# Layer one's first product by seven half-width products in blocks 2 to 5, with the weights for it fetched piece by piece into two buffers

## The chip, the cores and the metric

One core of a Trainium2 chip runs the kernel. The metric is the device time of one execution in microseconds; less is better. The core's engines work at the same time, each through its own instructions in a fixed order: PE (TensorE, matrix products), DVE (VectorE), ACT (ScalarE), POOL (GpSimd) and SP, which here only issues transfers; ACT issues some as well. An engine that meets an instruction whose inputs or buffer are not ready waits, and so does all that stands behind it.

## The reference

Attention with a decay per head, in a running state, and then two feed-forward layers over all 3072 tokens (4 sequences of 768):

```python
for t in range(S):
    state = gamma[None, :, None, None] * state + np.einsum('bhd,bhe->bhde', k[:, :, t], v[:, :, t])
    y[:, :, t] = scale * np.einsum('bhd,bhde->bhe', q[:, :, t], state)
x = y.transpose(0, 2, 1, 3).reshape(B * S, H * D)
h = x @ moe_w_in;  x = np.maximum(0.01 * h, h) @ moe_w_out
h = x @ moe2_w_in; out = (h * np.cos(h)) @ moe2_w_out
```

The model width is 512 (8 heads of 64), the inner width of both layers 2048. All is float32.

## The kernel before

**Numbers in two parts.** Every operand of a large product is split into a high part that TensorE takes exactly and a low part. A product is then three matmuls (`mm3`, L360): high by high, low by high, high by low. A high part is a copy on ACT (`high_g`, L510), a low part a subtraction on DVE or POOL (`low_g`, L515). Layer weights come as 64-bit words, from which ACT, DVE and POOL make the two parts in four steps (`exponent`, `fraction`, `top_bits`, `round_up`, L123 to L139).

**Tiling.** The tokens form six blocks of 512 (`NB`, `BLK`), the inner width 16 tiles of 128 (`NF`), the model width 4 (`KD`). Attention goes by 24 units of 128 tokens (`C`), four to a block. A unit's matmuls (`excursion`, L406) use the PSUM banks p1 and p2 for the next unit's scores and state, and p3 for this unit's output.

**Layer one** is the loop over `SEGMENTS` (L765): blocks 0 and 1 in two parts each, while the weights are being made, then blocks 2 to 5 whole. For each tile f, `gemm1` (L487) multiplies the block by 128 columns of the first weights, 4 x 3 matmuls of 512 columns into one bank; ACT applies the slope (`Leaky.begin`, L502); `high_g` and `low_g` give the pair g; and some tiles later `gemm2_a` (L715) adds g times the second weights to four accumulators, 12 matmuls of 512 columns. The attention units of block n + 1 lie in block n (`block_steps`), two steps to a tile.

**Layer two** is the loop over 24 quads (L952). It multiplies pairs of token blocks and pairs of tiles by Strassen's seven products, `P1` to `P7`: seven products of sums of parts take the place of eight, and DVE adds the results together. The seven sums of weights for pair p are made ahead (`pair_at`, L603, `pair_sums`, L287), kept in DRAM (`w2i`) and fetched into the two large buffers b0 and b1 (`load_wi`, L351).

**What sets the order.** The order on each engine is that of the program. The preparation of layer two's weights and inputs is spread over blocks 2 to 5 by `Agenda` (L215): a step stands at a moment, and `tick` runs the moments, two to a tile. Transfers are nearly all issued by SP, in that order.

Of the kernel before, what the change touches and what calls it, by code (L numbers as in the profile page):

```python
# [60 lines left out]
XMADE = ("P1", "P2", "P3", "P5", "P7", "P6", "P4")  # L61

# [17 lines left out]
def body(ctx: ExitStack, tc: tile.TileContext, att, first, w1, w2, out):  # L80
# [128 lines left out]
    xq = [[dpool.tile([P, 1024], F32, name=f"xq{s}_{i}") for i in range(14)] for s in range(1, NB // 2)]  # L209
# [87 lines left out]
    def xprep(agenda, m, s, xlow=None, step=13):  # L297
# [9 lines left out]
        for k in range(2):  # L307
            way = {}
            for i, name, keep in ((0, "P1", True), (1, "P2", True), (3, "P3", True), (0, "P5", False), (2, "P7", False), (3, "P6", False), (1, "P4", False)):
                j = 7 * k + XMADE.index(name)  # L310
                if s == 0:
                    way[name] = parts(place(i), partial(own_x, j), 0, xlow or nc.vector, keep, None)
                else:
                    way[name] = parts(place(i), xq[s - 1][j], 0, nc.vector, keep, ostage, False)
# [17 lines left out]
    def load_xq(s, j):  # L332
        assert ("x", s) in made
        xt[j] = w_tile(j, 0, F32R, 1024)
        nc.sync.dma_start(out=xt[j].bitcast(F32), in_=xq[s - 1][j])

    def own_x(j):
        if j not in xt:
            xt[j] = w_tile(j, 0, F32R, 1024)
# [9 lines left out]
    wi = {}  # L349

    def load_wi(p, place):  # L351
        assert ("p", p) in made
# [127 lines left out]

    def new_x(n):
# [37 lines left out]
    with tc.manual_schedule():  # L519

        with ExitStack() as pctx, ExitStack() as actx:
# [4 lines left out]
            xs = {}  # L526
# [11 lines left out]
            def evacuate(u):  # L538
                n = u // CPB
                if n not in xs:  # L540
# [8 lines left out]
            def unit_steps(u):  # L549
                def both():  # L550
# [3 lines left out]
                    heads.lower[u](nc.gpsimd)  # L554
# [12 lines left out]
                return [both, int, state, int, values, int, int, int]  # L567

            def block_steps(n):
                return [step for u in range(n * CPB, n * CPB + CPB) for step in unit_steps(u)]  # L570

            agenda = Agenda()
            START, LAST = 4, 2 * (NF * (NB - 3) - 4)
            m, turn = 0, 0
# [4 lines left out]
            def raw2():  # L582
                return cbuf[:, 0:2, :].rearrange("p a n -> p (a n)")

            def begin(f, part):
                return lambda: fetch2(raw2(), f, part)

            def half(f):
# [453 lines left out]
```

## Time and profile before

| what | us |
|---|---|
| median of 3 runs | 1099.12 (1098.64 to 1100.45) |
| the profiled execution | 1098.76 |
| its span, first to last instruction | 1096.9 |
| PE busy | 1080.1 (98%) |
| DVE busy | 658.9 (60%) |
| ACT busy | 484.3 (44%) |
| POOL busy | 179.7 (16%) |

The stages of the profiled execution: the start up to 35 us, blocks 0 and 1 to 219.5, blocks 2 to 5 to 595, layer two to the end. Busy shares are means over these stages. Matmuls overlap in the records, so the distance from one start to the next tells more of them than how long each lasts. The chain of work is followed backwards from the last instruction, at each step to what released it; an engine with a large share of it sets the time. Transfers move 189 MB in all.

### The profile page before, as it was taken

How to read it: one execution, taken by the hardware profiler on the slowest of the kernel's cores; microseconds unless marked ns; L12 is line 12 of the kernel's file. 1: busy time of each engine (PE TensorE's matmuls, PEld its weight loads, DVE VectorE, ACT ScalarE, POOL GpSimd, SP SyncE). 2: the span in 40 equal slices, each digit the busy share in tenths (PEclk: the TensorE clock that was granted, in tenths of full speed). 3: DMA queues.
4: the chain of work that ended last, by engine and by line, in shares of the span. 5: the costliest groups of instructions: out<-in, count | busy, mean ns of one | idle time of the engine just before them, and what ended most of it. 6: DMA issues, size and time to landing. Idle time of an engine off the chain costs nothing.

```text
span 1096.9 us, 18667 instructions
## 1 busy us (share of the span) xinstructions
PE 1080.1 (98%) x7484; PEld 897.4 (82%) x7484; DVE 658.9 (60%) x1003; ACT 484.3 (44%) x826; POOL 179.7 (16%) x146
## 2 busy tenths in 40 slices
PE   6899999999999999999999999999999999999998
PEld 6788888888888888888888888888888888888887
DVE  4788843123544535343786777877667877656665
ACT  3468732223434434343553555544445544444432
POOL 3210011112534333341464000000000000000000
PEclk9999999999999999999999999999999999999999
DMA  8646433133646445433795446585446495413412
GB/s 314 237 147 229 163 92 101 41 116 118 195 134 219 145 154 183 154 106 115 249 332 187 156 162 239 172 308 211 161 168 240 159 329 199 163 68 146 167 43 77
DMA packets 71082, 189.22 MB, mean 173 GB/s; under 512 B 7891, under 2 KB 10195, under 8 KB 70995
## 3 DMA queue, kind: packets, MB, share of 16 engines
q1 hardware_dynamic: 67536, 175.44, 46.1%
q10 hardware_dynamic: 3456, 12.58, 3.4%
q8 instruction: 59, 0.97, 0.4%
q14 instruction: 31, 0.23, 0.1%
HBM read 135.57 MB, written 52.43 MB: 171 GB/s over the span
## 4 chain that ended last, share of the span: by engine, by line
PE 96%; DMA 3%; issue 0%; ACT 0%; POOL 0%; SPq 0%; ACTq 0%; DVE 0%; POOLq 0%
PE p L361 19%; PE p L363 19%; PE p L362 19%; PE acc L361 12%; PE acc L362 12%; PE acc L363 12%; PE p L412 3%; DMA w<-att 2%; PE p L415 1%; DMA vs<-att 0%; PE acc L412 0%; ACT vp L400 0%; POOL vp L402 0%; PE p L492 0%; PE p L493 0%
## 5 line engine op out<-in xcount | busy, mean ns | idle before, releaser
L361 PE MATMUL acc<-g,w 128*128 128x512 f32 x384 | 151.3, 394 | 0.0
L363 PE MATMUL acc<-g,w 128*128 128x512 f32 x384 | 149.6, 390 | 0.0
L362 PE MATMUL acc<-g,w 128*128 128x512 f32 x384 | 149.6, 389 | 0.0
L361 PE MATMUL p<-b,w 128*128 128x512 f32 x380 | 148.1, 390 | 0.0
L363 PE MATMUL p<-b,w 128*128 128x512 f32 x380 | 147.8, 389 | 0.0
L362 PE MATMUL p<-b,w 128*128 128x512 f32 x380 | 147.8, 389 | 0.0
L361 PE MATMUL p<-w,b 128*128 128x512 f32 x336 | 130.7, 389 | 0.0
L362 PE MATMUL p<-w,b 128*128 128x512 f32 x336 | 130.7, 389 | 0.0
L363 PE MATMUL p<-w,b 128*128 128x512 f32 x336 | 130.7, 389 | 0.0
L516 DVE TENSOR_TENSOR g<-t,g 128x512 fp32r<-128x512 f32 x96 | 84.7, 885 | 53.4 <-ACT g L512 53.4
L504 ACT ACTIVATE t<-p 128x512 f32<-128x512 f32 x96 | 57.3, 597 | 121.8 <-PE p L363 114.4
L361 PEld LDWEIGHTS acc<-g,w 128*128 128x128 f32 x384 | 72.1, 188 | 15.6
L363 PEld LDWEIGHTS acc<-g,w 128*128 128x128 f32 x384 | 72.1, 188 | 15.2
L362 PEld LDWEIGHTS acc<-g,w 128*128 128x128 f32 x384 | 72.1, 188 | 14.6
L363 PEld LDWEIGHTS p<-b,w 128*128 128x128 f32 x380 | 71.3, 188 | 14.9
L362 PEld LDWEIGHTS p<-b,w 128*128 128x128 f32 x380 | 71.3, 188 | 14.8
L361 PEld LDWEIGHTS p<-b,w 128*128 128x128 f32 x380 | 71.3, 188 | 14.8
L512 ACT CAST g<-t 128x512 fp32r<-128x512 f32 x96 | 59.4, 619 | 53.5 <-PE acc L363 53.2
L860 ACT ACTIVATE k<-d,bias 128x512 int32<-128x512 f32 x24 | 17.4, 726 | 141.9 <-DVE d L847 141.9
L865 ACT ACTIVATE r<-r,bias 128x512 f32<-128x512 f32 x96 | 69.6, 725 | 18.4 <-DVE r L862 18.4
L362 PE MATMUL p<-w,w 128*128 128x512 f32 (+1 forms) x196 | 75.4, 385 | 0.0
L363 PE MATMUL p<-w,w 128*128 128x512 f32 (+1 forms) x196 | 75.4, 385 | 0.0
(133 smaller groups left out, 2043.3 us busy)
## 6 DMA issues: line engine op xcount, KB each, us to landing
b<-w2i SPq DMA_DIRECT2D x60, 512.0 KB, 5.7
w<-w2d SPq DMA_DIRECT2D x32, 512.0 KB, 8.1
w<-xq SPq DMA_DIRECT2D x28, 512.0 KB, 5.5
cbuf<-w SPq DMA_DIRECT2D x24, 512.0 KB, 4.0
xq<-o SPq DMA_DIRECT2D x40, 256.0 KB, 2.3
vs<-att SPq DMA_DIRECT2D x17, 512.0 KB, 3.8
w<-w SPq DMA_DIRECT2D x16, 512.0 KB, 10.1
w<-w ACTq DMA_DIRECT2D x16, 512.0 KB, 4.6
```

The source lines that it names most:

```text
L361: nc.tensor.matmul(o, sh, mh, start=start, stop=False)
L362: nc.tensor.matmul(o, sl, mh, start=False, stop=False)
L363: nc.tensor.matmul(o, sh, ml, start=False, stop=stop)
L412: return lambda: nc.tensor.matmul(out, stationary, moving, start=True, stop=True)
L415: return lambda start, stop: nc.tensor.matmul(out, stationary, moving, start=start, stop=stop)
L504: nc.scalar.activation(out=t, in_=hp, func=AF.Prelu, alpha=0.01)
L512: nc.scalar.copy(out=pair[:, 0], in_=g)
L516: eng.tensor_tensor(out=pair[:, 1], in0=g, in1=pair[:, 0].bitcast(F32), op=ALU.subtract)
L860: nc.scalar.activation(out=k, in_=h, func=AF.Identity, bias=bias[:, 0:1], scale=1.0)
L865: nc.scalar.activation(out=r, in_=r, func=AF.Sin, bias=bias[:, 1:2], scale=TURN)
```

## The change

In blocks 2 to 5 the tiles are taken in pairs, and layer one's first product is computed as layer two's is: by seven products, here of 256 columns (half a block of tokens), each 2 x 3 matmuls. `first_layer(i)` does pair i of 32; DVE adds the results in two tiles of the tag `t`, ACT applies the slope there, and POOL makes the low part for one of the two tiles of a pair. The bank pairs in `WHERE` put two products into each bank, and odd pairs use the banks in another order than even ones.

What this needs is made elsewhere. `first_pair` makes the sums of layer one's weights for a pair of tiles, from the parts already in SBUF, in blocks 0 and 1, and keeps them in DRAM (`w1i`). `x_steps` makes the seven sums of a block's inputs; for it the attention units of blocks 2 to 5 leave their tokens unsplit (`plain_tokens`). `follow` and `load_wi` fetch the weights of pair i + 2 in four pieces on ACT's queue, after pair i, into eight tiles of the first weights that are no longer needed; layer two's weights go the same way. Pairs run forwards in one block and backwards in the next, so that two pairs at each turn stay.

The agenda has four moments to a pair; the units and the steps of `x_steps` stand at moments of their own (`plan`). Six pairs of layer two's weights instead of four are made up to block 4, from two buffers by turns, with the low parts on DVE. The inputs of layer two's first two blocks go in part through DRAM and are fetched at the end of block 5, and layer two's input and weight tiles change places. The core of the diff:

```diff
+HALF = BLK // 2
+WHERE = ({"P1": (0, 0), "P6": (0, 1), "P7": (1, 0), "P5": (1, 1), "P2": (3, 0), "P4": (3, 1), "P3": (2, 0)},
+         {"P1": (1, 0), "P6": (1, 1), "P7": (3, 0), "P5": (3, 1), "P2": (0, 0), "P4": (0, 1), "P3": (2, 0)})
+WSLOTS = ((2, 3, 4, 5), (9, 10, 11, 12))
+RAW = (0, 1)
+XSLOTS = ((6, 7, 8), (13, 14, 15))
+XSHARED = {0: (("P1", 0), ("P1", 1), ("P6", 0), ("P6", 1)), 1: (("P4", 0), ("P4", 1), ("P3", 0), ("P3", 1))}
+XLATE = (*XSHARED[1], ("P2", 1))
+XALONE = {("P7", 0): 0, ("P7", 1): 1, ("P5", 0): 6, ("P5", 1): 7, ("P2", 0): 8, ("P2", 1): 13}
...
+    turns = [("a", pair_of(q)) for q in range(NQ * (NB - 2))] + [("p", pair_of(q)) for q in range(NQ * NB // 2)]
+
+    def follow(i, eng=nc.sync):
+        if i + 2 < len(turns) and turns[i + 2] not in wi:
+            return load_wi(turns[i + 2], wi[turns[i]][1], eng)
+        return []
+
+    def load_wi(key, place, eng=nc.sync):
+        assert key in made
         for old in [o for o in wi if wi[o][1] == place]:
             del wi[old]
-        t = xpool.tile([P, 4096], F32R, tag=f"b{place}", name=f"b{place}")
-        wi[p] = t, place
-        for lo, hi in ((0, 1024), (1024, 2048), (2048, 3072), (3072, WIN)):
-            nc.sync.dma_start(out=t[:, lo:hi].bitcast(F32), in_=w2i[p][:, lo:hi])
+        src = (w1i if key[0] == "a" else w2i)[key[1]]
+        tiles = []
+        wi[key] = tiles, place
+
+        def piece(i):
+            n = min(1024, WIN - 1024 * i)
+            t = w_tile(WSLOTS[place][i], 0, F32R, 1024)
+            eng.dma_start(out=t[:, :n].bitcast(F32), in_=src[:, 1024 * i : 1024 * i + n])
+            tiles.append(t)
+
+        return [partial(piece, i) for i in range(4)]
...
+        def plain_tokens(self, u, raw, tok0):
+            for j in range(2):
+                nc.vector.tensor_tensor(
+                    out=raw[j].rearrange("p (k n) -> p k n", k=2)[:, :, tok0 : tok0 + C],
+                    in0=self.po[u][:, j * 256 : j * 256 + 256].rearrange("p (k n) -> p k n", k=2),
+                    in1=self.tb[:, O_Q + j * 256 : O_Q + j * 256 + 256].rearrange("p (k n) -> p k n", k=2),
+                    op=ALU.mult,
+                )
...
+            when = {8: -37, 9: -28, 10: -21, 11: -15}
+            plan = {}
+            for u in range(2 * CPB, NU):
+                t = when.setdefault(u, 8 * (u - 3 * CPB) - 2)
+                both, state, values = unit_steps(u)
+                plan.setdefault(t, []).append(both)
+                plan.setdefault(t + 1, []).append(state)
+                plan.setdefault(t + 2, []).append(values)
+            for n in range(2, NB):
+                t = when[n * CPB + 3]
+                for at, fn in zip((-7, -4, 2, 3, 4, 4, 6) if n > 2 else (3, 4, 6, 10, 10, 10, 11), x_steps(n)):
+                    plan.setdefault(t + at, []).append(fn)
...
-                first, mid, last = rounding(raw2, t)
-                high, low = parts(t, w2d[f], 0, nc.gpsimd, False, ostage)
-                for i, step in zip((0, 2, 3, 3, 4, 5), (begin(f, 1), first, mid, last, high, low)):
+                first, mid, last = rounding(partial(raw2, turn), t)
+                high, low = parts(t, w2d[f], 0, nc.vector, False, ostage)
+                for i, step in zip((1, 3, 4, 5, 5, 6), (begin(f, 1, turn), first, mid, last, high, low)):
...
+                def plain():
+                    send(w1i[p][:, 0:1024], w()[0].bitcast(F32), False)
+                    for i in range(2):
+                        send(w1i[p][:, 3072 + 256 * i : 3328 + 256 * i], w()[1][:, 256 + 512 * i : 512 + 512 * i].bitcast(F32), False)
+
+                def whole():
+                    for i in range(2):
+                        sub2(held(i), w()[i][:, :512], w()[i][:, 512:], ALU.add)
+
+                highs = late_fn(lambda: w_tile(2 * p, 0, F32, 1024) if way == "own" else heads.first)
+
+                def room(i):
+                    return lambda n: highs()[:, 512 * i : 512 * i + 512]
+
+                g2 = parts(partial(held, 0), w1i[p], 1024, nc.gpsimd, False, room(0), False)
+                g3 = parts(partial(held, 1), w1i[p], 2048, nc.vector, False, room(1), False)
+                agenda.put(b, plain, whole)
+                agenda.put(b + 1, lambda: pair_sums(held(0), held(1)))
+                agenda.put(b + 2, g2[0], g3[0])
+                agenda.put(b + 3, g2[1], g3[1], lambda: made.add(("a", p)))
...
+            for p, (b, way) in enumerate(zip((-42, -26, -20, -23, -18, -16, -14, -7), ("own", "own", 3, 0, 1, 2, 4, 5))):
+                first_pair(p, b - 2 * START, way)
+            agenda.put(-6 - 2 * START, lambda: at_once(load_wi(("a", 0), 0)))
+            agenda.put(-7 - 2 * START, lambda: at_once(load_wi(("a", 1), 1)))
...
+            def first_layer(i):
+                n, q = 2 + i // NQ, i % NQ
+                key = turns[i]
+                p = key[1]
+                first, second = (stage("t") for _ in range(2))
+                a, b, c, d = first[:, :HALF], first[:, HALF:], second[:, :HALF], second[:, HALF:]
+                banks = {}
+
+                def product(name):
+                    at, half = WHERE[q % 2][name]
+                    if half == 0:
+                        banks[at] = bank(at)
+                    o = banks[at][:, half * HALF : half * HALF + HALF]
+                    x = xin[n, name]
+                    for k in range(2):
+                        h, l = w_part(key, name, k)
+                        mm3(o, h, l, x[:, k * HALF : k * HALF + HALF], x[:, 512 + k * HALF : 512 + k * HALF + HALF], k == 0, k == 1)
+                    if (n, q) == (NB - 1, NQ - 1) and name == "P5":
+                        load_xq(0, "P3", 1)
+                    if (n, q) == (NB - 1, NQ - 1) and name == "P2":
+                        load_xq(0, "P2", 1)
+                    return o
+
+                def moment(j):
+                    at = 4 * i + j
+                    for step in plan.pop(at, ()):
+                        step()
+                    flush()
+                    agenda.run(at - 2 * START)
+                    at_once(arriving[j : j + 1])
+
+                def add(out, o, s):
+                    nc.vector.tensor_tensor(out=out, in0=o, in1=s, op=ALU.add)
+
+                def slope(t):
+                    nc.scalar.activation(out=t, in_=t, func=AF.Prelu, alpha=0.01)
+
+                def ready(t, g, f, k):
+                    pending.append((gemm2_q, n, f, low_g(t, g, nc.gpsimd if k else nc.vector), (q, k) == (0, 0), (q, k) == (NQ - 1, 1)))
+
+                p1, p6 = product("P1"), product("P6")
+                nc.vector.tensor_copy(out=a, in_=p1)
+                add(b, p6, a)
+                p7, p5 = product("P7"), product("P5")
+                add(c, p7, b)
+                add(d, p5, c)
+                add(b, p5, b)
+                p2, p4 = product("P2"), product("P4")
+                add(a, p2, a)
+                add(c, p4, c)
+                slope(second)
+                add(b, product("P3"), b)
+                arriving = follow(i, nc.scalar)
+                g = high_g(second)
+                slope(first)
+                moment(0)
+                fn, *args = pending.pop(0)
+                fn(*args)
+                ready(second, g, 2 * p + 1, 0)
+                moment(1)
+                moment(2)
+                while len(pending) > 1:
+                    fn, *args = pending.pop(0)
+                    fn(*args)
+                ready(first, high_g(first), 2 * p, 1)
+                moment(3)
```

How this changes the order at three places. PE in block 2 ahead of the change, where one tile's first product ends and a second product of block 1, two tiles late, begins:

```order
1051 L361 MATMUL p_2644<-b_1880,w_0_684 128x512
1052 L362 MATMUL p_2644<-b_1880,w_0_684 128x512
1053 L363 MATMUL p_2644<-b_1880,w_0_684 128x512
1054 L361 MATMUL acc_2077<-g,w_1_1776 128x512
1055 L362 MATMUL acc_2077<-g,w_1_1776 128x512
1056 L363 MATMUL acc_2077<-g,w_1_1776 128x512
```

PE in the first pair of block 2 now, from P4 to P3 (`p_2808` is the bank of P2 and P4, `p_2824` that of P3):

```order
1027 L413 MATMUL p_2808<-w_0_2626,w_0_2603 128x256
1028 L414 MATMUL p_2808<-w_0_2626,w_0_2603 128x256
1029 L415 MATMUL p_2808<-w_0_2626,w_0_2603 128x256
1030 L413 MATMUL p_2824<-w_0_2529,w_0_2599 128x256
1031 L414 MATMUL p_2824<-w_0_2529,w_0_2599 128x256
1032 L415 MATMUL p_2824<-w_0_2529,w_0_2599 128x256
```

Where 12 matmuls of 512 columns stood for each tile, 42 of 256 columns stand for two tiles, and a second product follows only behind all seven. DVE in block 3 ahead of the change, from one low part of g (L516) to the next unit's mask (L448); L129 and L134 work on layer two's weights:

```order
281 L516 TENSOR_TENSOR g<-t,g 128x512
282 L129 TENSOR_SCALAR cbuf<-cbuf 128x512
283 L134 SCALAR_TENSOR_TENSOR cbuf<-cbuf 128x512
284 L461 TENSOR_TENSOR state<-p_3676,state 128x256
285 L516 TENSOR_TENSOR g<-t,g 128x512
286 L129 TENSOR_SCALAR cbuf<-cbuf 128x512
287 L134 SCALAR_TENSOR_TENSOR cbuf<-cbuf 128x512
288 L516 TENSOR_TENSOR g<-t,g 128x512 x2
289 L129 TENSOR_SCALAR cbuf<-cbuf 128x512
290 L134 SCALAR_TENSOR_TENSOR cbuf<-cbuf 128x512
291 L448 TENSOR_TENSOR sf<-p_3909,first 128x512
```

DVE in an early pair of block 2 now: the eight operations of the seven products (L1047, L1038), then the low part (L577), an attention unit and layer two's weights:

```order
306 L1047 COPY t<-p_3216 128x256
307 L1038 TENSOR_TENSOR t<-p_3216,t 128x256
308 L1038 TENSOR_TENSOR t<-p_3231,t 128x256 x3
309 L1038 TENSOR_TENSOR t<-p_3247,t 128x256 x2
310 L1038 TENSOR_TENSOR t<-p_3263,t 128x256
311 L138 TENSOR_SCALAR cbuf<-cbuf 128x512
312 L143 SCALAR_TENSOR_TENSOR cbuf<-first,cbuf 128x512
313 L577 TENSOR_TENSOR g<-t,g 128x512
314 L500 TENSOR_TENSOR sf<-p_3298,first 128x512
315 L513 TENSOR_TENSOR state<-p_3299,state 128x256
316 L535 TENSOR_TENSOR w_0_2748<-p_3300,first 128x2x128
317 L535 TENSOR_TENSOR w_0_2749<-p_3300,first 128x2x128
```

Eight short operations on PSUM have come in for each pair, with one low part of g between them instead of two. ACT around one fetch of layer two's weights (L124 and L126 are its first steps) ahead of the change:

```order
264 L512 CAST g<-t 128x512
265 L504 ACTIVATE t<-p_3528 128x512
266 L124 ACTIVATE cbuf<-cbuf 128x512
267 L126 ACTIVATE cbuf<-cbuf 128x512
268 L512 CAST g<-t 128x512
269 L504 ACTIVATE t<-p_3567 128x512
270 L268 CAST o<-cbuf 128x512
271 L706 ACTIVATE o<-acc_2701 128x512
```

ACT in the first pair of block 2 now (L1041 is the slope, L573 a high part, L398 a piece of weights from `w1i`):

```order
214 L1041 ACTIVATE t<-t 128x512
215 L573 CAST g<-t 128x512
216 L1041 ACTIVATE t<-t 128x512
217 L398 DMA w_0_2838<-w1i_118 128x1024
218 L398 DMA w_0_2861<-w1i_118 128x1024
219 L133 ACTIVATE cbuf<-cbuf 128x512
220 L135 ACTIVATE cbuf<-cbuf 128x512
221 L398 DMA w_0_2865<-w1i_118 128x1024
222 L573 CAST g<-t 128x512
223 L398 DMA w_0_2905<-w1i_118 128x512
```

The pieces of layer one's weights stand between the steps of layer two's weights, and some of them behind L133, which waits for a fetch.

## Rows read from the trace of the kernel before

**Rows 1.** Busy time on the page: busy us (share of the span) x instructions.
```profile
PE 1080.1 (98%) x7484; PEld 897.4 (82%) x7484; DVE 658.9 (60%) x1003; ACT 484.3 (44%) x826; POOL 179.7 (16%) x146
```

**Rows 2.** Shares of the chain that ended last, on the page, by engine.
```profile
PE 96%; DMA 3%; issue 0%; ACT 0%; POOL 0%; SPq 0%; ACTq 0%; DVE 0%; POOLq 0%
```

**Rows 3.** PE's waits from 60 us on: total us, times, longest.
```profile
PE p L415 <- ACT t L504: 0.4, 1, 0.4
```

**Rows 4.** Stretches: us, busy PE, PEld, DVE, ACT, POOL (instructions), PEclk, DMA share, GB/s.
```profile
85.40:145.20 59.80, 59.80 (x265) 49.46 (x264) 52.54 (x89) 43.67 (x85) 0.66 (x1) 1.00 0.47 161
...
219.50:316.20 96.70, 96.28 (x881) 79.67 (x880) 36.43 (x54) 33.74 (x58) 29.63 (x24) 1.00 0.44 145
316.20:412.30 96.10, 96.10 (x882) 79.62 (x881) 42.14 (x59) 38.28 (x67) 38.13 (x30) 1.00 0.49 162
412.30:508.30 96.00, 96.00 (x834) 79.54 (x832) 40.87 (x59) 38.13 (x67) 34.44 (x26) 1.00 0.46 151
508.30:595.30 87.00, 87.00 (x385) 72.07 (x384) 60.35 (x66) 43.37 (x80) 45.74 (x30) 1.00 0.67 234
```

**Rows 5.** Matmuls near the end, in order: start us, us.
```profile
1090.48 0.39 PE L363 MATMUL p<-w,w 128*128 128x512 f32 x1
1090.70 0.28 PE L361 MATMUL p<-w,w 128*128 128x256 f32 x1
1090.82 0.28 PE L362 MATMUL p<-w,w 128*128 128x256 f32 x1
1090.94 0.28 PE L363 MATMUL p<-w,w 128*128 128x256 f32 x1
```

**Rows 6.** Matmuls around one attention unit in block 2: start us, us.
```profile
270.69 0.39 PE L363 MATMUL p<-b,w 128*128 128x512 f32 x1
...
273.03 0.50 PE L361 MATMUL acc<-g,w 128*128 128x512 f32 x1
```

**Rows 7.** DVE's groups in 219.5 to 595.3 us: busy us, mean ns | idle before.
```profile
L516 DVE TENSOR_TENSOR g<-t,g 128x512 fp32r<-128x512 f32 x64 | 62.0, 971 | 29.1 <-ACT g L512 29.1
...
L461 DVE TENSOR_TENSOR state<-p,state 128x256 f32<-128x256 f32 x19 | 8.0, 420 | 3.0 <-PE p L415 2.4 <-PE p L412 0.6
...
L275 DVE TENSOR_TENSOR po<-t,po 128x256 fp32r<-128x256 f32 x4 | 5.4, 1354 | 6.3 <-ACT po L268 6.3
```

**Rows 8.** DVE in order, blocks 0 and 1: start us, us.
```profile
128.66 0.69 DVE L145 TENSOR_TENSOR w<-cbuf,w 128x512 fp32r<-128x512 f32 x1
129.28 0.68 DVE L516 TENSOR_TENSOR g<-t,g 128x512 fp32r<-128x512 f32 x1
129.88 0.42 DVE L129 TENSOR_SCALAR cbuf<-cbuf 128x512 int32<-128x512 int32 x1
130.33 0.69 DVE L134 SCALAR_TENSOR_TENSOR cbuf<-w,cbuf 128x512 int32<-128x512 int32 x1
```

**Rows 9.** DVE's groups in 60 to 219 us.
```profile
L516 DVE TENSOR_TENSOR g<-t,g 128x512 fp32r<-128x512 f32 x29 | 20.7, 716 | 20.3 <-ACT g L512 20.3
```

**Rows 10.** ACT's groups over the span.
```profile
L512 ACT CAST g<-t 128x512 fp32r<-128x512 f32 x96 | 59.4, 619 | 53.5 <-PE acc L363 53.2
```

**Rows 11.** POOL's groups in 219.5 to 595.3 us.
```profile
L275 POOL TENSOR_TENSOR cbuf<-cbuf,o 128x512 fp32r<-128x512 f32 x16 | 21.2, 1324 | 8.0 <-ACT o L268 8.0
```

**Rows 12.** Waits in 219.5 to 595.3 us: total us, times, longest.
```profile
DVE cbuf L129 <- ACT cbuf L124: 56.1, 20, 6.0
...
ACT cbuf L124 <- DMA cbuf<-w: 36.8, 16, 3.6
```

**Rows 13.** Transfers in 508.3 to 595.3 us: issues, KB each, median us to landing.
```profile
b<-w2i SPq DMA_DIRECT2D x6, 512.0 KB, 6.5
```

**Rows 14.** Stretches of 10 us, columns as in Rows 4.
```profile
560.00:570.00 10.00, 10.00 (x46) 8.29 (x45) 6.08 (x12) 4.97 (x10) 4.47 (x3) 1.00 1.03 412
570.00:580.00 10.00, 10.00 (x46) 8.29 (x45) 9.60 (x9) 6.63 (x13) 8.49 (x5) 1.00 1.03 402
590.00:600.00 10.00, 10.00 (x46) 8.29 (x45) 3.73 (x5) 3.12 (x6) 0.59 (x1) 1.00 0.82 288
```

More of the change, by code (lines that the diff above doesn't have):

```diff
@@ L310, in xprep @@
                 j = 7 * k + XMADE.index(name)
-                if s == 0:
+                if s == 0 and (name, k) not in XLATE:
                     way[name] = parts(place(i), partial(own_x, j), 0, xlow or nc.vector, keep, None)
                 else:
-                    way[name] = parts(place(i), xq[s - 1][j], 0, nc.vector, keep, ostage, False)
+                    way[name] = parts(place(i), xq[s][j], 0, nc.vector, keep, ostage, False)
             b = m + step * k
@@ L525, in body, with x_piece @@
             NU = B * NCH
-            xs = {}
+            xs, raws, xin = {}, {}, {}
+            def x_piece(n, name):
+                if (n, name) not in xin:
+                    if name in ("P1", "P6", "P7", "P5"):
+                        b = xpool.tile([P, 4096], F32R, tag=f"b{n % 2}", name=f"b{n % 2}")
+                        xin.update(((n, at), b[:, 1024 * i : 1024 * i + 1024]) for i, at in enumerate(("P1", "P6", "P7", "P5")))
+                    else:
+                        xin[n, name] = w_tile(XSLOTS[n % 2][("P2", "P4", "P3").index(name)], 0, F32R, 1024)
+                return xin[n, name]
@@ L539, in evacuate @@
                 n = u // CPB
+                if n > 1:
+                    if n not in raws:
+                        raws[n] = [w_tile(i, 0, F32, 1024) for i in RAW]
+                    heads.plain_tokens(u, raws[n], u % CPB * C)
+                    return
                 if n not in xs:
@@ L713, in body, with first_pair, held @@
             sums = {}
+            spot = late_fn(lambda: xpool.tile([P, 4096], I32, tag="b0", name="b0"))
+            def first_pair(p, b, way):
+                w = late_fn(lambda: [wslot["a", 2 * p + i, 0] for i in range(2)])
+                def held(i):
+                    if way == "own":
+                        return heads.first[:, 512 * i : 512 * i + 512].bitcast(I32)
+                    return spot()[:, way * 1024 + i * 512 :][:, :512] if way < 4 else cbuf[:, (way - 4) * 2 + i, :]
+                def plain():
[14 more added lines that the diff above has]
+                agenda.put(b + 3, g2[1], g3[1], lambda: made.add(("a", p)))
@@ L764, in body @@
             leaky = Leaky()
-            for seg, (n, f0, f1) in enumerate(SEGMENTS):
-                limit = LAG - 2 if seg < 4 else 1
+            for seg, (n, f0, f1) in enumerate(SEGMENTS[:4]):
+                limit = LAG - 2
                 steps = list(PLAN[seg])
@@ L817, in body @@
+            plan_closed = []
+            for i in range(NQ * (NB - 2)):
+                first_layer(i)
+                if 4 * i + 3 >= 95 and not plan_closed:
+                    plan_closed.append(1)
                     actx.close()
@@ L940, in after_group @@
                 load_wo(f, places[f])
-        places = {f: f for f in range(8)}
+        places = {f: NF - 1 - f for f in range(8)}
         xagenda = Agenda()
@@ L954, in unit @@
                 if q == 0:
-                    fn, *args = left[i]
-                    fn(*args)
+                    for fn, *args in pending[i : i + 1]:
+                        fn(*args)
                 elif i < 2:
@@ L993, in body @@
             spare()
-            if q + 2 < QUADS and pair_of(q + 2) not in wi:
-                load_wi(pair_of(q + 2), wi[pair_of(q)][1])
+            at_once(follow(NQ * (NB - 2) + q))
             if q > 0:
```

178 lines of the change are left out of this document (120 added, 58 removed).

## The prediction

> **What bounds the kernel now.** I read the busy shares first: PE is busy for 1080.1 of 1096.9 us [rows 1]. A busy PE need not bind, so the chain of work that ended last comes next: 96% of it is PE, the rest almost all the loads at the start [rows 2]. Then what PE waited for: from 60 us to the end there is one wait, 0.4 us [rows 3]. So the time is the number of matmuls times their spacing, and the clock adds nothing: the granted clock is 1.00 in the stretches I use, its upper level of 2.4 GHz [rows 4]. A matmul of 512 columns lasts 0.39 us and one of 256 columns 0.28 us, but they overlap; what counts is start to start. That is 0.227 us for 512 columns (1090.48 to 1090.70; over longer rows 0.2267) and 0.120 us for 256 (1090.70, 1090.82, 1090.94) [rows 5]. The very form that the change uses, 128x128 weights against 256 columns, is thus in the trace: 24 of them at the end.
>
> **What the change takes out and puts in on PE.** Layer one's first product in blocks 2 to 5 is 4 blocks x 16 tiles x 12 = 768 matmuls of 512 columns: 768 x 0.2267 = 174.1 us. In its place stand 4 x 8 pairs x 7 products x 6 = 1344 matmuls of 256 columns: 1344 x 0.1200 = 161.3 us. The difference is **-12.8 us**. Seven eighths of the columns alone would give 21.8 us; a spacing of 0.120 instead of 0.1133 (half of 0.2267) takes 9.0 of them back. Everything else on PE (the second product, the attention units, layer two) has the same count in both orders. A pair now takes 42 x 0.120 + 24 x 0.2267 = 10.5 us, against 10.9 before, and 2.1 us more where an attention unit lies (270.69 to 273.03, less one matmul) [rows 6]; 32 pairs and 11 units come to 359 us, 11.2 a pair.
>
> Of the price of a narrow matmul the rows show 0.120 us. The Trainium skill (TensorE: Matmul & The Clock Gate, Back-to-back issue gap) states N/2.4 + 2.5 ns for the warm gap, 109 ns here and 216 ns for 512 columns; by that the same counts would give 165.7 - 146.8 = 19.0 us. The trace disagrees at both widths (120 and 227), so I take the rows.
>
> **What it adds on DVE.** Eight operations of 128x256 that read PSUM per pair; such a form takes 0.42 us [rows 7]. It also moves the low parts of layer two's weights from POOL to DVE, takes the tokens' low parts off POOL, and gives POOL half of g's low parts. I counted the changed order between the first and the last pair: 316 operations that read PSUM and 224 that read SBUF alone. DVE starts the next one 0.61 us after one of 0.69 (128.66, 129.28, 129.88) and 0.45 after one of 0.42 on SBUF [rows 8]; for 256 columns of PSUM I take 0.345 (0.42 less the same 0.08). That gives 113 + 120 = 233 us. Operations on SBUF alone get longer while POOL works: g's low part takes 0.716 us on average ahead of block 2 and 0.971 in blocks 2 to 5 [rows 7, 9]. POOL has 88 operations left there, of 24 + 30 + 26 + 30 = 110 before [rows 4], so I keep that 0.255 us for each: 224 x 0.255 = 57 us. DVE then has 290 us of work in 359, 81%: not the bound on average, but much nearer than now (36.4 of 96.7 us in block 2 [rows 4]). Cost on average: nothing, under PE's 10.5 us.
>
> The cover is thin in single pairs. The heaviest is the seventh of block 3, with 8 and 16 operations: 2.8 + 8.4 + 4.1 = 15.2 us against PE's 10.5, so DVE enters the next pair 4.7 us late. PE does not feel that at once: all products of a pair fit into four PSUM banks that were emptied long before. It waits when the attention unit behind the next second product wants the banks of that pair's own products: PE comes there 5.04 + 2.72 = 7.8 us after the pair's start, DVE is through with the eight at 4.7 + 2.8 = 7.5. What exceeds 0.3 us falls on PE one for one. If collisions cost nothing PE waits for nothing, if they cost twice as much it waits 3.8 us there and 1.6 us in block 2, whose seventh pair has 1.7 us to spare. Bounds for such waits: 0 to 6 us; I take **+1 us**, near the middle case's zero.
>
> **In-order queues.** Each pair's add of P7 now waits until POOL has made the last pair's second low part, since both use one buffer. The high part ahead of it takes ACT 0.62 us [rows 10] and the g buffer that the next second product frees, 2.7 us after P3; POOL's low part takes 1.32 us [rows 11]. With 1 us for what else ACT has, that ends 5.7 us after P3; the add comes after 5.4 + 2.9 = 8.3. ACT waits for a fetch of layer two's weights for up to 3.6 us [rows 12], and the weight pieces of layer one and the slopes now stand behind that wait: DVE is 1.0 us late then, inside the cover above. The weights are fetched piece by piece, four per pair on ACT's queue, each in pair i for pair i+2, so the first piece has 16 us; such fetches land in 6.5 us even in the stretch with most transfers [rows 13]. Cost: 0.
>
> **Ahead of block 2.** DVE is busy for 52.5 of 59.8 us in block 0's second part [rows 4]. The first pair's sums (3.2 us) and two attention units (4.0) come into it, 7.2 us against 7.3 free, and PE gets the units' 4.2 us there too. Bounds 0 to 2 us, taken 0. The loads into layer two (2.6 MB behind the last products, 16 us or more ahead of the first quad's P2, P4 and P3): 0 to 3 us, taken 0.
>
> **Sum.** The profiled execution took 1098.76 us (span 1096.9 and 1.9 around it), 0.36 below the median of 1099.12. 1098.76 - 12.8 + 1 = 1086.9; on the median's footing **1087.3 us**.
>
> **Rivals.**
> *Transfers bind in block 5.* The changed program moves 256 MB, not 188. In block 5 I count 32.0 MB in 83.8 us, 382 GB/s. For: in 590 to 600 us the rate was 288 GB/s at a share of 0.82, so 351 when full [rows 14]; 32.0/0.351 = 91 us, 7 us more, and the time 1094. Against: 412 and 402 GB/s were moved in 560 to 580 us at a full share [rows 14], PE not waiting [rows 3], and 32.0 MB at 407 take 79 us. Also the weights have ACT's queue, while most of the backlog would be in SP's, whose loads are wanted later.
> The Trainium skill (SBUF — State Buffer, Summary: rules for kernel authors) says to reckon with about 358 GB/s between HBM and SBUF; by that block 5 would be 5.5 us too long. The 20 us at over 400 speak against it here.
> *The queues couple and PE waits a little, often.* For: DVE waits 56 us for ACT and ACT 37 us for fetches in these blocks already [rows 12], and each now has less slack. If half of the 24 pairs that carry the preparation of layer two's weights lose 0.5 us, that is 6 us: 1093; the case covers 1089.5 to 1097.
> *DVE becomes the bound, and the kernel slower.* An operation on SBUF that meets POOL's can be held for long: the four of 128x256 on `po` take 1.354 us, 0.9 more than undisturbed [rows 7]. At 7 a pair, DVE's 7.3 us reach PE's mean of 11.2 when 4.3 of 7 are held like that; the gain is eaten at 12.8/24 = 0.53 us a pair more, 4.9 of 7. At 5.6 of 7 DVE needs 12.3 us, 26 us more in 24 pairs: 1112. Against: a mean of 0.971 stands for under 0.3 us each, and POOL has less to do.
> *Narrow matmuls cost no fixed part.* At half of 0.2267 the gain is 21.8 us: 1077. The 24 rows speak against it. The Trainium skill's formula (TensorE: Matmul & The Clock Gate, above) would give 1080.
> *The gain is eaten.* New waits of 12 us, such as a late start of block 2, leave 1099.
>
> **How the numbers follow.** Forecast (PE's sum with up to 3 us of waits, 1085 to 1089.5): 0.55. Coupled queues: 0.20, of it 0.18 below 1096.9. Transfers: 0.08. DVE the bound: 0.09. Narrow matmuls cheaper: 0.03. Gain eaten: 0.05. The range of 1085 to 1096 holds the forecast, the transfers and most of the coupled case, about 0.8; its low end is the sum without any wait, 1085.9, less the spread of the runs. A measurement here can tell about 0.2%, 2.2 us, from no change. Faster: 0.55 + 0.18 + 0.08 + 0.03 = 0.84; same 0.02 + 0.05 = 0.07; slower 0.09.
>
> **What will show it.** Right: narrow matmuls 0.120 us apart in blocks 2 to 5, pairs 10.5 us apart without a unit, PE's waits after 60 us under 3 us, DVE busy for 75 to 90% there. Wrong: PE waiting for DVE at the units or at the first product of a pair (DVE, queues), PE waiting for a transfer into the weights' tiles or a stretch of block 5 at a full share with PE idle (transfers), another spacing (the first term).

## The result, and the profile after

The changed kernel takes **1115.11 us** (median of 4 runs, 1111.11 to 1116.38) where the kernel before took 1099.14 beside it: a ratio of **1.0136 [1.0123, 1.0149]**, slower by 16 us. The prediction was 1087.3, in a range of 1085 to 1096. The profiled execution took 1111.11 us with a span of 1109.3.

Busy shares and chain of the page, to be held against [rows 1, 2]:

```profile
PE 1078.5 (97%) x8060; PEld 919.9 (83%) x8060; DVE 784.2 (71%) x1381; ACT 500.9 (45%) x854; POOL 152.8 (14%) x132
...
PE 76%; DMA 10%; DVE 6%; ACT 3%; issue 2%; POOL 1%; SPq 1%; ACTq 0%; POOLq 0%; DVEq 0%
```

PE's share of the chain fell from 96% to 76%, and 10% of it are now transfers, 3% before. The five largest waits of PE from 60 us on, where [rows 3] was one wait of 0.4 us (three more come to 1.9 us):

```profile
PE p L467 <- DVE t L1038: 5.8, 6, 1.9
PE acc L413 <- DVE o L850: 3.5, 2, 2.7
PE p L413 <- DMA w<-w1i: 1.7, 1, 1.7
PE acc L413 <- ACT o L848: 0.8, 1, 0.8
PE acc L413 <- ACT g L573: 0.7, 1, 0.7
```

L467 is the attention unit, waiting for DVE to empty the banks of the pair's own products (L1038 is an add of such a product); L413 on `acc` is a second product whose accumulators have not been evicted (L850, L848) or whose high part is late (L573). The stretches of blocks 2 to 5 in the columns of [rows 4] (us, busy PE, PEld, DVE, ACT, POOL, PEclk, DMA share, GB/s):

```profile
224.70:323.30 98.60, 96.66 (x1053) 86.71 (x1052) 69.80 (x139) 39.67 (x69) 30.18 (x25) 1.00 0.82 281
323.30:420.60 97.30, 94.23 (x1025) 84.50 (x1024) 66.88 (x145) 42.19 (x76) 30.95 (x26) 1.00 0.83 290
420.60:518.50 97.90, 94.02 (x849) 83.36 (x848) 66.24 (x140) 40.64 (x73) 27.19 (x22) 0.98 0.76 259
518.50:609.80 91.30, 86.41 (x530) 77.35 (x529) 58.60 (x119) 37.59 (x67) 21.88 (x16) 0.98 0.91 328
```

DVE is busy for 64 to 71% of them and is not the bound. What has changed most is the DMA share: 0.76 to 0.91, where it was 0.44 to 0.49 in blocks 2 to 4 and 0.67 in block 5. Twelve of the 32 pairs last longer than the 10.5 us (12.75 with a unit) that their matmuls take, by 0.4 to 4.6 us each, 21.6 us in all; the other twenty have those lengths to 0.01 us (the first of them 2.72 more, for a third second product).

One of the twelve in order of time, on four engines (start us, us; in brackets the idle time before and what ended it). `first` holds raw weights of layer two, the `cbuf` slot that L133 writes is a buffer for rounded weights, `w2d` is where such weights are written out:

```profile
273.71 0.90 SPq L257 DMA_DIRECT2D first<-w  x1
274.70 0.58 SPq L247 DMA_DIRECT2D w2d<-cbuf  x1
```
```profile
273.44 0.61 ACT L609 CAST w<-w 128x512 fp32r<-128x512 f32 x1
282.89 0.66 ACT L133 ACTIVATE cbuf<-first 128x512 f32<-128x512 f32 x1 [8.84 <-DMA w2d<-cbuf]
...
284.02 0.62 ACT L1041 ACTIVATE t<-t 128x512 f32<-128x512 f32 x1
284.67 0.62 ACT L573 CAST g<-t 128x512 fp32r<-128x512 f32 x1
```
```profile
285.32 1.42 DVE L577 TENSOR_TENSOR g<-t,g 128x512 fp32r<-128x512 f32 x1 [0.58 <-ACT g L573]
...
291.61 0.42 DVE L1047 COPY t<-p 128x256 f32<-128x256 f32 x1
292.06 2.77 DVE L1038 TENSOR_TENSOR t<-p,t 128x256 f32<-128x256 f32 x7
```
```profile
293.89 0.27 PE L467 MATMUL p<-sf,vp 64*64 64x64 f32 x2 [1.02 <-DVE t L1038]
```

ACT stands for 8.84 us at the exponent (L133), the first step of layer two's weights, until a buffer has been written out. Behind it in ACT's order stand the slope (L1041) and the high part (L573) of layer one. DVE begins g's low part at 285.32, has the tokens' low parts and the weights' sums before it, and copies the pair's first product at 291.61, though the pair began at 284.45. The unit at 293.89 has waited for one of the adds behind it. ACT's holds at L133 in these blocks were, where [rows 12] shows 36.8 us in 16 waits of at most 3.6:

```profile
ACT cbuf L133 <- DMA w2d<-cbuf: 20.9, 3, 8.8
ACT cbuf L133 <- DMA first<-w: 18.8, 5, 8.4
```

The sum of the waits is hardly larger; but most of it now comes as five single holds of 6 to 9 us. Landing times, in the columns of [rows 13], are longer too (over 224 to 612 us; the kernel before had 4.0 for raw weights and 3.1 for the write-out there):

```profile
first<-w SPq DMA_DIRECT2D x14, 512.0 KB, 7.5
...
w2d<-cbuf SPq DMA_DIRECT2D x16, 256.0 KB, 6.2
```

The shares above are means over blocks of some 95 us. While ACT is held, the share of the stretches of 2 us from 274 to 280 us is 0.91, 0.91 and 1.04; the last of them, in the columns of [rows 4]:

```profile
278.00:280.00 2.00, 2.00 (x15) 1.83 (x14) 1.44 (x4) 0.00 (x0) 1.04 (x1) 1.00 1.04 417
```

### The profile page after: what moved, and what is told of

Its sections match the earlier page's. It is cut to its first block, busy times and chain, and to the rows that moved or that the text cites. A ratio compares the mean times of both kernels' runs of the same rounds, so it can differ in the third digit from the quotient of the medians.

```text
span 1109.3 us, 20610 instructions
## 1 busy us (share of the span) xinstructions
PE 1078.5 (97%) x8060; PEld 919.9 (83%) x8060; DVE 784.2 (71%) x1381; ACT 500.9 (45%) x854; POOL 152.8 (14%) x132
## 4 chain that ended last, share of the span: by engine, by line
PE 76%; DMA 10%; DVE 6%; ACT 3%; issue 2%; POOL 1%; SPq 1%; ACTq 0%; POOLq 0%; DVEq 0%
PE p L413 15%; PE p L415 15%; PE p L414 15%; PE acc L413 9%; PE acc L415 9%; PE acc L414 9%; PE p L464 2%; DMA w2d<-cbuf 2%; DMA first<-w 2%; DVE t L1038 1%; POOL g L577 1%; DMA vs<-att 1%; DMA w<-w 1%; DMA cbuf<-w 1%; DMA w<-w2d 1%
## 5 line engine op out<-in xcount | busy, mean ns | idle before, releaser
L413 PE MATMUL p<-b,w 128*128 128x512 f32 (+1 forms) x572 | 195.9, 342 | 0.5 <-DVE t L1038 0.5
L415 PE MATMUL p<-b,w 128*128 128x512 f32 (+1 forms) x572 | 195.4, 342 | 0.0
L414 PE MATMUL p<-b,w 128*128 128x512 f32 (+1 forms) x572 | 195.4, 342 | 0.0
L413 PE MATMUL p<-w,w 128*128 128x512 f32 (+1 forms) x532 | 186.0, 350 | 1.7 <-DMA w<-w1i 1.7
L415 PE MATMUL p<-w,w 128*128 128x512 f32 (+1 forms) x532 | 185.7, 349 | 0.0
L414 PE MATMUL p<-w,w 128*128 128x512 f32 (+1 forms) x532 | 185.7, 349 | 0.0
L413 PE MATMUL acc<-g,w 128*128 128x512 f32 x384 | 152.9, 398 | 5.0 <-DVE o L850 3.5
L413 PEld LDWEIGHTS p<-b,w 128*128 128x128 f32 x572 | 108.3, 189 | 14.6 <-DVE t L1038 0.9
L414 PEld LDWEIGHTS p<-b,w 128*128 128x128 f32 x572 | 108.3, 189 | 13.3
L415 PEld LDWEIGHTS p<-b,w 128*128 128x128 f32 x572 | 108.3, 189 | 12.4
L413 PEld LDWEIGHTS p<-w,w 128*128 128x128 f32 x532 | 100.7, 189 | 15.2 <-DMA w<-w1i 1.9
L415 PEld LDWEIGHTS p<-w,w 128*128 128x128 f32 x532 | 100.7, 189 | 13.0
L414 PEld LDWEIGHTS p<-w,w 128*128 128x128 f32 x532 | 100.7, 189 | 12.9
L1038 DVE TENSOR_TENSOR t<-p,t 128x256 f32<-128x256 f32 x224 | 84.4, 419 | 24.1 <-POOL g L577 14.9
L413 PEld LDWEIGHTS acc<-g,w 128*128 128x128 f32 x384 | 72.6, 189 | 21.1 <-DVE o L850 4.3
L1041 ACT ACTIVATE t<-t 128x512 f32<-128x512 f32 x64 | 40.3, 629 | 94.7 <-DVE t L1038 91.5
```

Source lines behind the costliest of these rows:

```text
L413: nc.tensor.matmul(o, sh, mh, start=start, stop=False)
L414: nc.tensor.matmul(o, sl, mh, start=False, stop=False)
L415: nc.tensor.matmul(o, sh, ml, start=False, stop=stop)
L1038: nc.vector.tensor_tensor(out=out, in0=o, in1=s, op=ALU.add)
L1041: nc.scalar.activation(out=t, in_=t, func=AF.Prelu, alpha=0.01)
```

## The experiments

Theory A: too many transfers; each lands later, ACT is held in order, the slopes behind it come late, DVE falls behind, PE waits. Theory B: DVE's own load and its collisions with POOL make DVE late. Each experiment edits the changed kernel except where the kernel before is named; times are medians.

**Without the repeated fetches.** Edit, in `load_wi`:

```
+            if key[0] == "a":
+                wi[key] = wi.pop(old)
+                return []
             del wi[old]
```

> Leaves out the 44 MB of layer one's weight sums that the change fetches again for each pair: every pair after the second uses the tiles of the first two pairs, so layer one's weights are the wrong ones, and PE, DVE, ACT and POOL have the same instructions. Theory A (too many transfers: each lands later, ACT is held in order at the exponent of layer two's weights, the slopes and DVE's low parts behind it come late, PE waits at the units): the fetches land in about 4 us as before, ACT's holds at the exponent fall from 40 us in all to under 15, PE's waits from 25 us to under 8, time 1087 to 1095. Theory B (DVE's own load and its collisions with POOL make DVE late, transfers have no part): same work on DVE and POOL, so 1108 to 1116.

Measured: 1090.39 us, 0.9914 [0.9899, 0.9929] of the kernel before, 24.7 us less than the change, with the same 8060 matmuls and the same work on DVE and POOL. B falls, and DVE was busy for no less without the transfers (789.6 us against 784.2), so the transfers don't make its work longer either. One figure of A is missed: ACT's holds at the exponent don't fall under 15 us but to 26.9, one of them still 7.0 us long, while PE's waits fall to 1.1 us. The edit removes the volume, but also ACT's issues of these fetches and their waits for PE to free a tile; the next one parts the two.

**The same fetches, cut to 16 columns.**

```
-            t = w_tile(WSLOTS[place][i], 0, F32R, 1024)
+            t = kept[i] if kept else w_tile(WSLOTS[place][i], 0, F32R, 1024)
+            n = 16 if kept else n
```

> The change, its 24 repeated fetches cut to the first 16 of each piece's 1024 columns, into the tiles that the pair before left there (wrong weights from the third pair on): the same DMA instructions at the same places of ACT's stream, with the same waits for PE to free a tile and the same engines' work, without the volume (43 of 44 MB less). If the volume is what costs: as without the fetches, 1088 to 1094. If the place of the issues on ACT's stream costs the 8 us that SP's queue gave: 1096 to 1101. If the issues were nearly all of it: over 1104.

Measured: **1088.68 us**, 0.9904 [0.9887, 0.9920]. With the volume 26.4 us of the change's time go; the issues, still at their places, cost nothing by themselves. PE's waits from 60 us on, all of them, and two landing times:

```profile
PE acc L415 <- DVE o L852: 1.3, 1, 1.3
PE p L469 <- DVE t L1040: 0.2, 1, 0.2
```
```profile
first<-w SPq DMA_DIRECT2D x14, 512.0 KB, 4.9
...
w2d<-cbuf SPq DMA_DIRECT2D x16, 256.0 KB, 2.7
```

The hold shown above stands here at the same place of ACT's order:

```profile
278.90 0.66 ACT L133 ACTIVATE cbuf<-first 128x512 f32<-128x512 f32 x1 [7.09 <-DMA w2d<-cbuf]
```

It is nearly as long, 7.09 us, and PE waits for nothing behind it. It ends 4.3 us before the next pair begins (at 283.20); in the change it ends 1.6 us before (282.89, 284.45). So a long hold of ACT is not a loss by itself: what counts is how late it ends against PE.

**The kernel before with added transfers.** In blocks 2 to 5, per tile, two copies (then one) within DRAM that nothing reads:

```
+                    if n > 1:
+                        for j in range(2):
+                            more = dpool.tile([P, 896], I32, name=f"more{n}_{f}_{j}")
+                            nc.scalar.dma_start(out=more, in_=w1[f].bitcast(I32)[:, 896 * j : 896 * j + 896])
```

> The kernel before, with 58.7 MB of additional transfers in blocks 2 to 5 that nothing reads (two copies of 448 KB within DRAM per tile, issued by ACT), the volume that the change fetches; nothing else is altered. If added transfers alone hold a kernel up (theory A in its widest form): landings lengthen to about 6 us, ACT's waits for fetches grow from 37 us to over 60, PE waits: 1104 to 1116. If it takes the change's thinner cover as well (heavier DVE, units that want banks of the same pair): 1098 to 1103.

> The kernel before with half of the additional transfers (29.4 MB, one copy of 448 KB per tile in blocks 2 to 5). If the loss goes with the volume: 1111 to 1117. If the first part of the added transfers falls into idle DMA time and only what is beyond it costs: 1099 to 1107.

Measured: 1129.33 us with two, ratio 1.0262 [1.0245, 1.0278], and 1106.40 with one, 1.0057 [1.0043, 1.0071]. (58.7 MB is a third more than the change's repeated 44 MB.) With two copies the time lies 13 us beyond the 1104 to 1116 of theory A. So the transfers need no heavier DVE and no thinner cover to do harm: the kernel before loses 29.8 us by them, with DVE busy for 151 of 390 us. The copies also stand in ACT's own order, some 0.5 us for each issue; no run here parts that from their volume. The same stretch of the kernel before, with one copy and with two; the second last number is the DMA share:

```profile
219.50:610.00 390.50, 390.07 (x3042) 323.06 (x3041) 185.87 (x247) 157.41 (x279) 147.95 (x109) 1.00 0.50 169
```
```profile
219.50:610.00 390.50, 384.98 (x3010) 317.92 (x3009) 175.03 (x240) 155.33 (x274) 147.22 (x109) 1.00 0.73 243
```
```profile
219.50:610.00 390.50, 375.32 (x2940) 307.04 (x2939) 151.09 (x226) 147.26 (x258) 136.17 (x103) 0.99 0.88 296
```

At a share of 0.73 it loses 6.4 us, at 0.88 29.8: half the volume costs a fifth. ACT's waits for raw weights (L124 there), 36.8 us before, are with two copies:

```profile
ACT cbuf L124 <- DMA cbuf<-w: 87.9, 23, 6.8
```

**Four buffers; earlier fetches; both.** The fourth pieces of both places share one tile, and the tile that is freed gives two more buffers for rounded weights; in the second edit the raw weights are fetched earlier.

```
-            t = w_tile(WSLOTS[place][i], 0, F32R, 1024)
+            t = w_tile(WSLOTS[place][i], 0, F32R, 1024) if i < 3 else fourth()[:, 512 * place : 512 * place + 512]
...
-                t = own(2 + turn % 2)
+                t = own()
```
```
-                for i, step in zip((1, 3, 4, 5, 5, 6), (begin
+                for i, step in zip((0, 3, 4, 5, 5, 6), (begin
-                times = (2, 3, 4, 4, 3, 4, 5, 5, 7, 8, 6, 7, 8, 9, 8, 10, 11)
+                times = (0, 3, 4, 4, 3, 5, 6, 6, 7, 8, 7, 8, 8, 9, 8, 10, 11)
```

> The same work, with four instead of two buffers for the rounded weights of layer two (the two new ones in a tile that the fourth weight pieces of both places no longer need), so the exponent need not wait until a buffer has been written out. Theory A: the three waits of 20.9 us for that write-out vanish, those of 18.8 us for raw weights stay; about half of the 25 us of PE's waits goes: 1099 to 1107. Theory B: nothing on DVE or POOL changes: 1111 to 1116.

> The same work, with layer two's raw weights fetched one moment (about 2.7 us) earlier in the halves, and in the pairs two moments earlier for the first fetch and one moment later use for the second; two buffers as in the change. Theory A: the waits of 18.8 us for raw weights fall under 6, those of 20.9 us for the write-out stay: 1101 to 1109. Theory B: 1111 to 1116.

> Both of the former: four buffers and the earlier fetches, all work and all transfers as in the change. Theory A in the form that the hold of ACT is the cause, whatever makes the transfers late: PE's waits fall under 8 us, 1088 to 1096, faster than both kernels. In the form that the transfers themselves are the limit: the waits move to another place (PE or SP waiting for layer one's weights), 1100 to 1110. Theory B: 1108 to 1116.

Measured: 1110.11 us (1.0088 [1.0071, 1.0104]), 1107.19 (1.0069 [1.0051, 1.0086]) and 1102.29 (1.0024 [1.0012, 1.0036]). The first misses A's 1099 to 1107, the second meets A's 1101 to 1109, the third the 1100 to 1110 for transfers as the limit. With four buffers alone the waits for the write-out went as expected, but ACT then came to the raw weights too early:

```profile
ACT w L133 <- DMA first<-w: 37.0, 9, 8.1
ACT cbuf L133 <- DMA cbuf<-w: 17.8, 6, 8.1
```

54.8 us in place of 18.8 and 2.8: one wait had covered the other. The earlier fetches alone cut the waits for `first<-w` to 6.2 us and leave 25.8 for the write-out. Both together give 12.8 us, about half of the 26.4 that go with the volume. My figure for the holds as the only cause, 1088 to 1096, is missed; but the holds had not gone, so this run can't say whether they are the only one:

```profile
ACT w L133 <- DMA first<-w: 26.2, 7, 6.0
```

Other places wait for a transfer as well, the eviction of block 4 among them, which wants a staging tile that is still being written out:

```profile
DVE o L865 <- DMA x2d<-o: 6.6, 1, 6.6
```

**Layer two's first tokens later.** On top of both:

```
-            xprep(agenda, 94, 0, step=18)
+            xprep(agenda, 97, 0, step=15)
```

> Four buffers and earlier fetches, and the preparation of layer two's first tokens three moments (8 us) later, so that its two staged parts don't want the four staging tiles in which block 4's four results go out at the same time (PE waited 2.3 us for an eviction there and lost 4.2 us in that pair). Theory A with this as a further place where work waits for a transfer to land: 3 to 5 us less than with four buffers and earlier fetches alone, 1097 to 1100. If the backlog of transfers merely moves: 1101 to 1104.

Measured: 1096.81 us, 0.9976 [0.9962, 0.9989], 5.5 less, just under the range for this: that wait is gone.

**The low part back on DVE.** `low_g(t, g, nc.gpsimd if k else nc.vector)` becomes `low_g(t, g, nc.vector)`.

> The change with one part undone: the low part of g of the second tile of each pair (32 operations) goes back from POOL to DVE, so that no P7 add waits for POOL, POOL collides less, and DVE has 32 more operations of 0.7 to 1.0 us. All transfers as in the change. Theory A (transfers): DVE was 65 to 71% busy and is not the bound, the holds of ACT stay: 1109 to 1119. Theory B (POOL's collisions and the wait for POOL make DVE late): the 14.9 us of the adds' waits for POOL vanish, under 1106.

Measured: 1123.27 us, 1.0209 [1.0194, 1.0224], 8 slower than the change and beyond what A had given. The 32 operations themselves add little (DVE is busy for 803 instead of 784 us, 71% of the span in both). What grew is DVE's standing in order for ACT's high part; these waits in the change, and here:

```profile
DVE g L577 <- ACT g L573: 19.9, 21, 3.0
```
```profile
DVE g L577 <- ACT g L573: 58.7, 38, 7.4
```

By these rows a late ACT holds DVE directly there; no run without the fetches tests it. POOL's part was a help in the change as it is.

**Weight pieces from SP's queue.** `follow(i, nc.scalar)` becomes `follow(i, nc.sync)`.

> The change with layer one's weight pieces issued by SP instead of ACT; same transfers and same work. If it was the issue of these fetches on ACT's own instruction stream that held ACT (a rival to A: a piece waits for PE to free its tile and the slopes stand behind it): 1098 to 1107. Theory A: the pieces stand behind SP's waits for ACT's high parts (120 us in all in these blocks) and come no sooner; ACT's holds at the exponent stay: 1110 to 1125.

Measured: 1107.38 us, 1.0060 [1.0039, 1.0082], 7.7 less than the change: A's figure is missed, the rival's nearly met. But the issues on ACT's stream are not the cause by themselves: the cut fetches keep every one of them and lose nothing. What moved is, in part, who lands late. In the change `w<-w1i` took 5.5 us, `first<-w` 7.5 and `w2d<-o` 6.1; here:

```profile
w<-w1i SPq DMA_DIRECT2D x72, 512.0 KB, 7.0
...
first<-w SPq DMA_DIRECT2D x14, 512.0 KB, 6.5
...
w2d<-o SPq DMA_DIRECT2D x16, 256.0 KB, 4.3
```

The pieces, which have two pairs of time, wait longer in the common queue, and some of the transfers for which ACT is held come sooner. Not all do: `cbuf<-w` stays at 6.3 us and `w2d<-cbuf` goes from 6.2 to 6.1, and ACT's holds at the exponent for transfers come to 45.6 us in all, no less than the change's 42.5, though the longest is 7.1 in place of 8.8. Which of these is worth the 7.7 us is not shown. The Trainium skill (DMA: Bandwidth & Descriptors, Queues, rings and completion order) says that each DMA engine takes turns between the queues that have work for it. The pieces' landing of 7.0 in place of 5.5 us is in line with that, since in SP's queue they no longer have turns of their own; no run here shows the turns. The Trainium skill's rule that spreading transfers over issuing engines doesn't help (DMA: Bandwidth & Descriptors, Rules for kernel authors) is one for bandwidth; the time of this kernel depended on the choice of the queue.

**All of these, and the sum's floor.** Four buffers, earlier fetches, later tokens, pieces from SP; and the first three without the repeated fetches.

> Four buffers, earlier fetches and later tokens as in the last experiment, and layer one's weight pieces issued by SP. If the issue of the pieces on ACT's stream and the short buffers are separate parts of the loss, the 8 us that SP's queue gave alone come on top in part: 1090 to 1095. If both relieve the same holds of ACT: 1095 to 1099, no difference that can be measured.

> Four buffers, earlier fetches and later tokens, and without the 44 MB of repeated weight fetches (wrong weights from the third pair on, same work on all engines). If nothing but the transfers stands between the change and PE's own sum: 1085 to 1088, PE's waits after 60 us under 3 us. If DVE's and POOL's load is a part of its own: 1089 to 1093.

Measured: **1092.87 us** (1091.35 to 1094.02), 0.9937 [0.9924, 0.9951], a version that beats both kernels with all the work done; and 1088.60, 0.9904 [0.9887, 0.9920], 0.6 above the range for "nothing but the transfers". That is the time of the cut fetches alone (1088.68): buffers, leads and later tokens are worth something only while the volume is there. In the former PE's waits from 60 us on are down to two:

```profile
PE p L423 <- DMA w<-w1i: 2.0, 1, 2.0
PE acc L423 <- DVE o L865: 1.6, 1, 1.6
```

and every pair but two has the length of its matmuls to within 0.12 us; the longest of the two holds the wait of 2.0 us for a weight piece.

## Why the prediction was wrong

*PE's term, -12.8 us: right.* Narrow matmuls lie 0.12 us apart in blocks 2 to 5 and undisturbed pairs take 10.50 us, 12.75 with a unit. With the volume of the fetches away the kernel takes 1088.7 us, 1.4 above the forecast, about as much as the 11 units cost beyond the 2.1 us that I had for each (2.25 us, 1.6 in all): the sum was that of a kernel whose transfers land in time.

*DVE, +1 us: near in size, not in its reasons.* I had DVE busy for 81%; it was 64 to 71%, and 73% where nothing else disturbs it. The pairs that I named as heavy lost next to nothing by themselves: with cut fetches PE waits 0.2 us for adds (its wait of 1.3 us for an eviction is at 106.7 us, ahead of block 2).

*In-order queues, 0: this is the step that failed.* Its working was a chain with 2.6 us of cover, against holds of ACT of "up to 3.6 us" [rows 12], read from the kernel before at DMA shares of 0.44 to 0.67 [rows 4]. The change moved that share to 0.76 to 0.91, and I had the volume in hand (256 MB, not 188), but used it only as throughput, and only for block 5. With the volume the raw weights landed in 6.3 and 7.5 us in place of 4.0 before, ACT's longest hold was 8.8 us in place of 3.6, and late landing, which the sum has at nothing, cost 26.4 us in all. (The weight pieces, for which it took 6.5 us from [rows 13], did land within that, in 5.5.) The step also passed over the second thing for which the exponent waits, a buffer's write-out, which was 20.9 of the 39.7 us at the two transfers above. And it priced a hold by its length: with the fetches cut, one of 7.09 us costs nothing, so the change gave ACT longer holds even without the volume, and the volume made them end too late.

*Ahead of block 2 and into layer two, 0 each: right.* With cut fetches block 2 starts at 223.5 us, about the 219.5 of before and the two units' 4.2; in the change at 224.7. In the change's layer two PE was busy for 474.99 of the 475 us from 610 on.

*The rivals.* "The queues couple and PE waits a little, often" had the mechanism, and by luck its count of pairs: 12 pairs lost time, but 1.8 us each on average in place of 0.5, so 21.6 us and not 6. "Transfers bind in block 5" came nearly true in its own block: it had 7 us, block 5 lost 7.3, of it 4.6 at an eviction that waited for a write-out and 2.0 at a weight piece, and the sign that was named for it, a full share with PE idle, is there ahead of that eviction (columns of [rows 4]):

```profile
536.00:538.00 2.00, 0.26 (x2) 0.00 (x0) 0.00 (x0) 0.00 (x0) 0.00 (x0) 1.00 0.99 380
```

That it is the eviction that waits was no part of it, and the other 14.3 of the 21.6 us were lost in blocks 2 to 4, at mean shares of 0.76 to 0.83, which it left out. "DVE becomes the bound" did not happen: putting work back on DVE cost 8 us, yet through ACT's lateness. That all three forms were priced separately, each with values from a quieter kernel, is why the slower side got 0.09.

*A further term, not in the prediction.* Of the 22.5 us between the spans of the change and of the kernel with cut fetches (1109.3, 1086.8) PE's idle time is 14.2; the other 8.3 are busy time, 1078.5 against 1070.2 for the same 8060 matmuls. The lower clock after two of the waits makes 3.4 us of that (rows in the last section). The other 4.9 are not traced here; some of it is how busy time is counted, since the last matmul ahead of a wait counts for its 0.39 us and not for the 0.227 after which the next could have begun [rows 5].

That the volume of the fetches is the cause is shown; the path from it over ACT and DVE to PE is read from traces, in one pair in full. What stays open is how the remaining loss of the version with four buffers and earlier fetches divides among its waits, what the choice of the queue changed, and how much of the loss by two copies (29.8 us, where the change loses 26.4 by its fetches) is their larger volume and how much their issue by ACT.

## What to carry to other kernels

A duration or a wait for a transfer that is read from a profile holds for that profile's DMA share: when a change adds volume, work out the new share for every stage first, and price each in-order wait for a transfer anew, before any sum. Leads and buffers that sufficed here at a mean share of 0.5 to 0.6 didn't at 0.8 to 0.9: a mean below 1 holds stretches at a full share, and a late landing hurts where an engine that serves the bound engine stands behind it. Of a hold ask when it ends against the bound engine, not only how long it is. Where volume has a long lead, try it in the queue of the urgent transfers, behind them: here that was worth 7.7 us, and 3.9 on top of buffers, leads and later tokens.

## What the runs showed of the hardware

*Landing times grow while the mean share is still below 1.* For 512 KB of raw weights the median was 4.0 us at a mean share of 0.50, 4.5 at 0.73 and 5.8 at 0.88 (kernel before, with one and two copies), and 6.3 to 7.5 in the change; the loss in the first three was 0, 6.4 and 29.8 us. Within such a mean, stretches of 2 us stood at 0.91 to 1.04 while ACT and PE waited (the rows at 278 and 536 us above).

*Two of PE's waits were followed by the lower clock.* Around the unit's wait of 1.86 us, which ended at 488.69, and after the one of 2.75 us, which ended at 539.01, the granted clock of stretches of 2 us is (third number from the end; then share and GB/s):

```profile
488.00:490.00 2.00, 1.31 (x32) 1.31 (x34) 1.64 (x5) 0.60 (x1) 0.00 (x0) 0.80 1.06 412
490.00:492.00 2.00, 2.00 (x39) 1.88 (x35) 0.94 (x2) 1.68 (x4) 0.00 (x0) 0.50 0.88 273
492.00:494.00 2.00, 2.00 (x8) 1.64 (x9) 2.00 (x5) 1.23 (x2) 0.00 (x0) 0.84 0.91 324
...
540.00:542.00 2.00, 2.00 (x7) 1.52 (x7) 1.80 (x6) 0.00 (x0) 0.00 (x0) 0.60 0.94 303
542.00:544.00 2.00, 2.00 (x7) 1.58 (x6) 1.91 (x5) 0.89 (x2) 0.00 (x0) 0.54 0.63 184
```

0.50 is the lower level, 1.2 GHz. What these stretches fall short of 1.00 by comes to 1.7 us each time, 3.4 in all. Waits of 1.33 us (up to 415.62) and 1.65 us (up to 571.28) were not followed by it: the stretches behind them show 1.00. At the lower level wide matmuls lie 0.43 us apart instead of 0.227:

```profile
541.00 0.63 PE L414 MATMUL acc<-g,w 128*128 128x512 f32 x1
541.42 0.63 PE L415 MATMUL acc<-g,w 128*128 128x512 f32 x1
541.85 0.63 PE L413 MATMUL acc<-g,w 128*128 128x512 f32 x1
```

The Trainium skill (TensorE: Matmul & The Clock Gate, Back-to-back issue gap) gives N/1.2 for the cold gap, 427 ns here; these rows agree. At the upper level the Trainium skill's figure for this width (same page and section), 216 ns, is below the 0.227 us of [rows 5]. In the kernel with cut fetches, whose two waits are 1.3 and 0.2 us, the granted clock is 1.00 from 224 to 610 us.
